# A gated linear-attention block: five small moves in the order of work around the Strassen query stage

## The chip, the core and the metric

The kernel runs on one core of a Trainium2 chip. Its time is device time in microseconds (us), from one launch, median of a few runs. In the profile, PE is the matrix engine (PEld its weight loads), DVE the vector engine, ACT the scalar engine, POOL the GpSimd engine, and SP the engine whose queue issues most DMAs. Each engine takes its own instructions strictly in order and waits on semaphores for the others.

## The reference

All tensors are float32: S = 2048 tokens, D = 640 features, 32 heads of 20, an MLP of width 1536.

```python
xn = layernorm(x)
q, k, v = split(xn @ wqkv)                       # 32 heads x 20
phi(p) = concat(softmax(p), softmax(-p))         # p = q or k times a 20x20 matrix per head
kv = phi_k^T v ;  z = sum_s phi_k                # per head
o = (phi_q kv) / (phi_q z + 1e-6)
s = o @ wo
g = silu(gelu(xn @ w1 + b1) @ w2 + b2)
out = x + s * g
```

## The kernel before

Float32 products are made from float32r parts: a number is split into a high part (copied by ACT) and a low part (original minus high), and a product is three matmul passes, high x high, high x low and low x high (`PASSES`). The head matrices are folded into wq and wk at the start.

**Stages.** (1) Loading and folding of weights, to about 45 us. (2) A loop over 16 token tiles t of 128 tokens, to about 212 us. (3) The Strassen query stage, `query_pair(q)` for q = 4 to 7, to about 250 us; it makes the queries of two tiles (2q and 2q + 1) with seven products instead of eight. (4) Twelve MLP units, each also Strassen, with the normalisation of stored query features beside them. (5) Numerators, output projection and gate.

**A step t of the tile loop** makes the key projection `pk = project(t, wk_s)` and the value projection `value(t)`. Each is 30 matmuls of 320 columns (line 363) into a PSUM tile `pA`, of which there are three; a projection can start when the readers of the tile that had its place are done. From `pk` comes the feature map:

- `feat1` on DVE: maximum (L376), minimum (L377), `p - max` into a slab `e` (L380, the last reader of `pA`), `nr = min - max` (L383); then on POOL the second half of `e` (L384).
- `feat2` on ACT: one exponential over 128x1280 (L393).
- `key_fin`: sums per head on DVE (L401), their reciprocal (L426), and the scaling of `e` on POOL (L406). The result is `phis[t]`.
- `kv_pair(t)`: 64 small matmuls of 40 columns for two tiles (L435), which add phi^T v into one PSUM tile `kv`. They read `phis` and `vs`.

`query(n)` does the same for a query tile, without `key_fin`, and stores `e` in DRAM (L420); queries 0 to 7 are made so, in steps 6 to 9.

**The x for pairs 4 to 7** comes transposed from DRAM (`xr`, 128x1280 for a pair) and is normalised in place: `pair_sub(q)` on POOL (L332), `pair_mul(q)` on DVE (L337). `pair_plain(q)` splits it: three copies on ACT (L283) and three subtractions on DVE (L285), into `xp` and a slab `b`. `t_sums(q)` on POOL (L298, five instructions) makes the Strassen sums `tt`, and `t_split(q)` splits them into `xd`: a copy on ACT (L314) and a subtraction of 128x1152 on POOL (L315).

**The query stage** has seven parts per pair, i = 0 to 6 (L616). Part 1 makes `qY`, which ACT copies (L622); part 3 makes `qV`, for which there is one PSUM place shared with `qY`. DVE adds results at parts 3, 4, 5 and 6 (L625, L627, L629, L632), and POOL adds once at part 1 (L623). After part i, `hooks[i]` runs, which is where the last tile's remaining key work and the making of the first MLP weights (`w1_forms`: L451, L462, L463) are put:

```python
            if i in hooks:
                hooks[i]()
```

Four weight tiles for this stage, `wqs`, are read back from DRAM by `s_back()` in step 15 (L587, on SP's queue).

**What sets the order.** The region is written under a manual schedule: every engine takes its instructions in the order in which the code above emits them. PSUM tiles and slabs are given out by pools; which place a tile gets, and so whom its first writer waits for, follows from the order of releases when the program is built.

Of the kernel before, what the change touches and what calls it, by code (L numbers as in the profile page):

```python
# [16 lines left out]
NT = S // P  # L17
# [18 lines left out]
def _tok(t):  # L36
    q, o = divmod(t, 2)
    h, p = divmod(q, SLOTS)
    return 8 * h + 4 * o + p
# [7 lines left out]
def hedgehog_gated_mlp_kernel(ctx: ExitStack, tc: tile.TileContext, x, xt_in, wqk, bd, wv, wo, w1, b1, w2, b2, out_t):  # L47
# [19 lines left out]
    def xd():  # L67
        if not xds:
            xds.append(xpool.tile([P, 9, 2, CW], F32R, tag="D", name="xd"))
        return xds[0]  # L70
# [10 lines left out]
    def slab(dt, name, shape=(P, 2, D)):  # L81
        return slabs.tile(list(shape), dt, tag="S", name=name)
# [4 lines left out]
    def bankA():  # L87
        return pools["A"].tile([P, 2, 512], F32, tag="A", name="pA")
# [179 lines left out]
    def at(q):  # L268
        return slice((q % SLOTS) * P, (q % SLOTS + 1) * P)
# [10 lines left out]
    def plain(q, o, v):  # L280
        parts = [(xp[:, 0:5, :, at(q)], v)] if o == 0 else [(beside(q), v[:, 0:2]), (xp[:, 5:8, :, at(q)], v[:, 2:5])]
        for dst, src in parts:
            nc.scalar.activation(dst[:, :, 0, :], src, AF.Copy)  # L283
        for dst, src in parts:
            nc.vector.tensor_tensor(dst[:, :, 1, :], src, dst[:, :, 0, :].bitcast(F32), op=OP.subtract)  # L285
# [26 lines left out]
    def t_split(q):  # L312
        tt, dst = tts.pop(q), xd()[:, :, :, at(q)]
        nc.scalar.activation(dst[:, :, 0, :], tt[:], AF.Copy)  # L314
        nc.gpsimd.tensor_tensor(dst[:, :, 1, :], tt[:], dst[:, :, 0, :].bitcast(F32), op=OP.subtract)  # L315
# [23 lines left out]
    def pair_plain(q):  # L339
        for o in range(2):  # L340
            plain(q, o, xrs[q][:, :, o * P:(o + 1) * P])
# [27 lines left out]
    def heads(ps):  # L369
        return ps[:, :, :HALF].rearrange("p a (h d) -> p a h d", d=DH)  # L370

    def feat1(ps, later=None):
        p4 = heads(ps)
        mx = small.tile([P, 2, 16], F32, tag="mx", name="mx")
        mn = small.tile([P, 2, 16], F32, tag="mn", name="mn")
        nc.vector.tensor_reduce(mx[:], p4, axis=AX.X, op=OP.max)  # L376
        nc.vector.tensor_reduce(mn[:], p4, axis=AX.X, op=OP.min)  # L377
        e = slab(F32, "e")[:]
        e5 = e.rearrange("p a (h s d) -> p a h s d", s=2, d=DH)
        nc.vector.tensor_tensor(e5[:, :, :, 0, :], p4, mx[:, :, :, None].to_broadcast([P, 2, 16, DH]),  # L380
                                op=OP.subtract)
        nr = small.tile([P, 2, 16], F32, tag="nr", name="nr")
        last_feat[0] = nc.vector.tensor_tensor(nr[:], mn[:], mx[:], op=OP.subtract)  # L383
        rest = lambda: nc.gpsimd.tensor_tensor(e5[:, :, :, 1, :], nr[:, :, :, None].to_broadcast([P, 2, 16, DH]),  # L384
                                               e5[:, :, :, 0, :], op=OP.subtract)
        if later is None:
            rest()
        else:
            later.append(rest)
        return e.rearrange("p a b -> p (a b)")  # L390

    def feat2(ef):
        nc.scalar.activation(ef, ef, AF.Exp)  # L393
        return ef

    def features(ps):
        return feat2(feat1(ps))

    def head_sums(ef, tag):
        ss = small.tile([P, 64], F32, tag=tag, name=tag)  # L400
        nc.vector.tensor_reduce(ss[:], ef.rearrange("p (g d) -> p g d", d=DH), axis=AX.X, op=OP.add)  # L401
        return ss
# [15 lines left out]
    def query(t):  # L418
        ef = features(project(t, wq_s))
        nc.scalar.dma_start(e_dram[_tok(t)], ef)  # L420
# [3 lines left out]
    def key_fin(ef):  # L424
        ss = head_sums(ef, "rc")
        nc.vector.reciprocal(ss[:], ss[:])  # L426
        scale_heads(ef, ss)
        return ef
# [10 lines left out]
    vs, es, phis, xns, wk_s, wq_s = {}, {}, {}, {}, [], [None] * 4  # L439
# [161 lines left out]
    def query_pair(q, hooks, later):  # L601
        even, odd = bankA(), None
        bank, seen = {"X": even[:, 0, :HALF], "W": even[:, 1, :HALF]}, set()
        r1 = row([P, 2, HALF], F32, "qx")
        r2 = row([P, 2, HALF], F32, "qu")
        for i, (ch, wn, xb, extra) in enumerate(QPARTS):
            if ch in "YV":
                bank[ch] = bankB("q" + ch)[:, :HALF]
            if i == 4:
                odd = bankA()  # L610
                bank["Z"] = odd[:, 0, :HALF]
            mms = [(wn, k, b, xb + k, a) for k in range(2) for a, b in PASSES]
            if extra:
                mms += [(extra[0], 0, b, extra[1], a) for a, b in PASSES]
            for n, (w, k, b, blk, a) in enumerate(mms):
                nc.tensor.matmul(bank[ch], q_x(blk, a, q), q_weight(w, k)[:, b], start=ch not in seen and n == 0,  # L616
                                 stop=n == len(mms) - 1, skip_group_check=True)
            seen.add(ch)
            if i == 0:
                nc.scalar.activation(r1[:, 0], bank["X"], AF.Copy)  # L620
            elif i == 1:
                nc.scalar.activation(r1[:, 1], bank["Y"], AF.Copy)  # L622
                nc.gpsimd.tensor_tensor(r2[:, 0], r1[:, 0], r1[:, 1], op=OP.add)  # L623
            elif i == 3:
                nc.vector.tensor_tensor(r2[:, 1], r2[:, 0], bank["V"], op=OP.add)  # L625
            elif i == 4:
                nc.vector.tensor_tensor(odd[:, 1, :HALF], r2[:, 1], bank["Z"], op=OP.add)  # L627
            elif i == 5:
                nc.vector.tensor_tensor(bank["W"], r2[:, 1], bank["W"], op=OP.add)  # L629
                ee = feat1(even)  # L630
            elif i == 6:
                nc.vector.tensor_tensor(bank["Z"], r2[:, 0], bank["Z"], op=OP.add)  # L632
            if i in hooks:
                hooks[i]()
        return ee, feat1(odd, later)

    def store_e(t, ef):
        nc.scalar.dma_start(e_dram[_tok(t)], feat2(ef))
# [9 lines left out]
    queries = iter(range(NT // 2))  # L648
# [3 lines left out]
    for t in range(6, NT):  # L652
        q = (t + 2) // 2
        pk = project(t, wk_s)
        for u in XIN.get(t, ()):
            x_in(u)
        for u in STATS.get(t, ()):
            pair_stats(u)
        if t in XR:
            load_xr(XR[t])  # L660
        if t in (6, 8):
            spill(t // 2 - 1)
        if t in (8, 10, 12):
            pair_sub(q)
        es[t] = feat1(pk)
        if t == 6:
            pair_stats(10)
            pair_sub(4)
            fold_w(wqT, range(4, KC), "wq", wq_s)
        if t in (6, 8, 10, 12):  # L670
            pair_mul(q)
        if t == 13:
            w1r = load_w1(0)
        if t in (7, 9, 11, 13):
            t_sums((t + 1) // 2)
        if t == NT - 1:
            s_back()
        if t == NT - 1:
            t_split(7)
        vs[t] = value(t)  # L680
        if t < NT - 1:
            feat2(es[t])
            phis[t] = key_fin(es.pop(t))
        if t in (8, 10, 12):
            pair_plain(q)
        if t in (7, 9):
            t_split((t + 1) // 2)
        if t == 12:
            t_split(6)
        if t == 6:  # L690
            query(next(queries))
            query(next(queries))
            pair_plain(4)
        if 7 <= t < 10:
            query(next(queries))
        if t % 2 == 0 and t < NT - 2:
            kv_pair(t - 2)
        if 7 <= t < 10:
            query(next(queries))
    w1f = w1_forms(w1r)  # L700

    def early_rest(q, ea):
        if q == 4:
            phis[NT - 1] = key_fin(es.pop(NT - 1))
        w1g.append(next(w1f))
        if q == 4:
            return
        later.pop(0)()
        store_e(2 * q - 2, ea)

    def late_rest(q, eb):
        if q == 7:
            w1g.append(next(w1f))
        if q > 4:
            store_e(2 * q - 1, eb)

    later, w1g, ea, eb = [], [], None, None
    for q in range(4, 8):
        if q == 7:
            w2r = [load_raw(w2[f * P:(f + 1) * P, :]) for f in range(GF)]  # L720
        ea, eb = query_pair(q, {1: lambda: early_rest(q, ea), 3: lambda: late_rest(q, eb), **({0: lambda: feat2(es[NT - 1])} if q == 4 else {})}, later)
        if q == 4:
            kv_pair(NT - 4)
        if q == 5:
            kv_pair(NT - 2)
            kvr = kv_rest()
# [494 lines left out]
```

## Time and profile before

| | |
|---|---|
| median of 3 runs | 661.41 us (661.08 to 661.45) |
| the profiled execution | 661.31 us, of which its span is 659.6 us |
| PE busy | 649.7 us (99%), 4414 matmul records |
| DVE, ACT, POOL busy | 486.5, 235.0, 390.5 us |
| mean granted PE clock | 0.999 |

In a row of the timeline the first number is the start in us from the span's start, the second the length of the row in us; then engine, line, operation, output and inputs, shapes, and how many instructions are merged in the row. Brackets tell how long the engine was idle just before, and what ended that idle time. The end of a matmul is modelled by the profiler, so a matmul row is best read by its start and by the start of the next one. A row of the waits has who waited for whom, the total in us, how often, and the longest.

### The profile page before, as it was taken

The page shows a single profiled execution, that of the slowest core. Times are in us where ns is not written, and L with a number is a line of the kernel's source. Part 1 is how long each engine was busy: PE and PEld are TensorE (multiplying, and loading weights), DVE is VectorE, ACT ScalarE, POOL GpSimd, SP SyncE. Part 2 cuts the span into 40 slices and gives each one's busy share as a digit, 9 for nine tenths or more (in the row PEclk, how much of TensorE's full clock was granted, in tenths as well). Part 3 has the DMA queues.
Part 4 walks back from the last instruction along what each step waited for, and adds up shares of the span by engine and source line. Part 5 has one row for each costly group of instructions (what it writes and reads, how often), then busy time and mean ns, then how long its engine had stood idle before and what let it go on. Part 6 is the DMA issues. An engine that isn't in the chain of part 4 may idle for free.

```text
span 659.6 us, 11407 instructions
## 1 busy us (share of the span) xinstructions
PE 649.7 (99%) x4414; PEld 564.1 (86%) x4414; DVE 486.5 (74%) x749; ACT 235.0 (36%) x334; POOL 390.5 (59%) x348
## 2 busy tenths in 40 slices
PE   9999999999999999999999999999999999999997
PEld 9999999999999898888888888888888887766866
DVE  5785955898686788668979968759789899852232
ACT  3512523233233346352442444841332424132130
POOL 2755464949566854957768876363472967343321
PEclk9999999999999999999999999999999999999999
DMA  9706092654204287537899799497779399999962
GB/s 351 272 1 172 6 329 108 157 175 137 82 15 147 88 277 264 173 95 264 190 294 314 171 408 327 97 318 258 151 218 242 84 260 201 303 230 244 280 235 81
DMA packets 161408, 132.22 MB, mean 200 GB/s; under 512 B 89170, under 2 KB 127314, under 8 KB 160458
## 3 DMA queue, kind: packets, MB, share of 16 engines
q1 hardware_dynamic: 158618, 119.89, 62.3%
q10 hardware_dynamic: 2736, 11.60, 4.8%
q8 instruction: 35, 0.57, 0.3%
q14 instruction: 19, 0.16, 0.1%
HBM read 83.74 MB, written 47.73 MB: 199 GB/s over the span
## 4 chain that ended last, share of the span: by engine, by line
PE 67%; DVE 8%; POOL 3%; ACT 1%; issue 1%; DMA 0%; DVEq 0%; POOLq 0%
PE pB L810 24%; PE pB L781 22%; PE pB L965 11%; PE pA L616 3%; PE pA L363 3%; PE pB L912 2%; POOL e L384 2%; DVE b L285 1%; DVE rc L401 1%; ACT e L393 1%; DVE xp L285 1%; DVE nr L383 1%; PE qV L616 1%; DVE mx L376 1%; DVE mn L377 1%
## 5 line engine op out<-in xcount | busy, mean ns | idle before, releaser
L810 PE MATMUL pB<-hs,w2s 128*128 128x512 f32 x720 | 165.7, 389 | 0.0
L810 PEld LDWEIGHTS pB<-hs,w2s 128*128 128x128 f32 x720 | 135.0, 188 | 28.8 <-DVE y L819 0.8
L781 PE MATMUL pB<-xp,w1s 128*128 128x512 f32 x324 | 81.3, 389 | 0.0
L781 PE MATMUL pB<-xd,w1s 128*128 128x512 f32 x324 | 79.3, 389 | 0.0
L965 PE MATMUL pB<-oT,wo 128*128 128x512 f32 (+1 forms) x315 | 72.3, 381 | 0.0
L781 PEld LDWEIGHTS pB<-xd,w1s 128*128 128x128 f32 x324 | 60.8, 188 | 12.6
L781 PEld LDWEIGHTS pB<-xp,w1s 128*128 128x128 f32 x324 | 60.7, 188 | 12.7 <-DVE pB L1046 0.2
L406 POOL TENSOR_TENSOR eq<-eq,rc 128x1280 f32<-128x1280 f32 x16 | 37.9, 2368 | 54.3 <-DVE rc L869 37.1
L965 PEld LDWEIGHTS pB<-oT,wo 128*128 128x128 f32 x315 | 57.2, 188 | 13.8 <-PE pB L912 2.5
L393 ACT ACTIVATE e<-e 128x1280 f32<-128x1280 f32 x32 | 40.7, 1272 | 75.0 <-POOL e L384 74.1
L819 DVE TENSOR_TENSOR y<-pB,y 128x512 f32<-128x512 f32 x100 | 63.2, 676 | 1.4 <-PE pB L810 1.4
L406 POOL TENSOR_TENSOR e<-e,rc 128x1280 f32<-128x1280 f32 x16 | 39.0, 2439 | 40.9 <-DVE rc L426 40.6
L384 POOL TENSOR_TENSOR e<-nr,e 128x640 f32<-128x640 f32 x32 | 43.8, 1370 | 31.4 <-DVE nr L383 24.3
L363 PE MATMUL pA<-wv,xp 128*128 128x320 f32 x384 | 59.8, 310 | 1.8 <-DVE nr L383 1.8
L786 ACT ACTIVATE pB<-pB,b1t 128x512 f32<-128x512 f32 x48 | 31.8, 662 | 78.9 <-DVE pB L1046 29.7
L363 PE MATMUL pA<-wk,xp 128*128 128x320 f32 x384 | 59.6, 310 | 0.0
L363 PEld LDWEIGHTS pA<-wv,xp 128*128 128x128 f32 x384 | 56.9, 188 | 2.1 <-issue 2.1
L363 PEld LDWEIGHTS pA<-wk,xp 128*128 128x128 f32 x384 | 56.9, 188 | 0.1
L856 POOL TENSOR_TENSOR ez<-eq,zrep 128x1280 f32<-128x1280 f32 x16 | 47.4, 2960 | 2.5 <-DMA eq<-e_dram 2.5
L463 POOL TENSOR_TENSOR w1s<-raw,w1s 128x640 fp32r<-128x640 f32 (+1 forms) x18 | 26.2, 1454 | 29.8 <-ACT w1s L462 29.8
L401 DVE TENSOR_REDUCE rc<-e 128x64 f32<-128x1280 f32 x16 | 23.7, 1483 | 23.5 <-ACT e L393 23.5
L968 POOL TENSOR_TENSOR xres<-gt,xres 128x256 f32<-128x256 f32 x20 | 14.3, 736 | 35.7 <-DVE gt L967 35.7
(165 smaller groups left out, 1102.7 us busy)
## 6 DMA issues: line engine op xcount, KB each, us to landing
raw<-in_w_dram SPq DMA_DIRECT2D x42, 320.0 KB
e_dram<-e ACTq DMA_DIRECT2D x16, 640.0 KB
eq<-e_dram SPq DMA_DIRECT2D x16, 640.0 KB
phi_t<-eq SPq DMA_DIRECT2D x64, 160.0 KB
phT<-phi_t SPq DMA_DIRECT2D x20, 480.0 KB
xres<-in_xt_dram SPq DMA_DIRECT2D x20, 256.0 KB
xt<-in_x_dram SPq DMA_DIRECT2D x15, 320.0 KB
out_dram<-xres SPq DMA_DIRECT2D x18, 256.0 KB
```

The lines of the kernel that those rows point to most:

```text
L363: nc.tensor.matmul(ps[:, hf, :HALF], stat_x(q, o, k, a), ws[k][:, b, hf * HALF:(hf + 1) * HALF], start=n == 0, stop=n == 3 * KC - 1)
L384: rest = lambda: nc.gpsimd.tensor_tensor(e5[:, :, :, 1, :], nr[:, :, :, None].to_broadcast([P, 2, 16, DH]), e5[:, :, :, 0, :], op=OP.subtract)
L393: nc.scalar.activation(ef, ef, AF.Exp)
L401: nc.vector.tensor_reduce(ss[:], ef.rearrange("p (g d) -> p g d", d=DH), axis=AX.X, op=OP.add)
L406: nc.gpsimd.tensor_tensor(e3, e3, rc[:, :, None].to_broadcast([P, 64, DH]), op=OP.mult)
L616: nc.tensor.matmul(bank[ch], q_x(blk, a, q), q_weight(w, k)[:, b], start=ch not in seen and n == 0, stop=n == len(mms) - 1, skip_group_che ...
L781: nc.tensor.matmul(bank[ch][:], tl[:, a, off + wo_:off + wo_ + P], mov(blk, b), start=new and n == 0, stop=n == len(mms) - 1, skip_group_c ...
L786: nc.scalar.activation(ps, ps, AF.Gelu_apprx_tanh, bias=b1t[:, f:f + 1])
L810: nc.tensor.matmul(ps[:], ws[i][:, b, d * P:(d + 1) * P], hs[o][i][:, a, :], start=i == n == 0, stop=(i, n) == (GF - 1, 2), skip_group_che ...
L819: nc.vector.tensor_tensor(y, ps[:], y, op=OP.add)
L856: nc.gpsimd.tensor_tensor(zv, ef, zf, op=OP.mult)
L965: nc.tensor.matmul(ps[:, mv], w, o[:, mv], start=n == 0, stop=n == 15, skip_group_check=True)
```

## The change

No instruction is added or removed; five groups move.

1. In steps 8, 10 and 12 `pair_plain(q)` stands before `key_fin(t)` instead of after it.
2. `t_split(6)` moves from the end of step 12 to step 13, behind `feat1`. `t_split(7)` moves from step 15 to step 14, behind `feat1`.
3. In step 8 the block of key-value matmuls `kv_pair(6)` moves behind the second query instead of between the two.
4. The last exponential, `feat2(es[15])`, moves from behind part 0 of `query_pair(4)` to behind part 1.
5. The last `key_fin` moves from behind part 1 to behind part 4.

```diff
         es[t] = feat1(pk)
+        if t in (13, 14):
+            t_split(t - 7)
...
-        if t == NT - 1:
-            t_split(7)
         vs[t] = value(t)
         if t < NT - 1:
             feat2(es[t])
-            phis[t] = key_fin(es.pop(t))
         if t in (8, 10, 12):
             pair_plain(q)
+        if t < NT - 1:
+            phis[t] = key_fin(es.pop(t))
         if t in (7, 9):
             t_split((t + 1) // 2)
-        if t == 12:
-            t_split(6)
...
         if 7 <= t < 10:
             query(next(queries))
+        if 7 <= t < 10:
+            query(next(queries))
         if t % 2 == 0 and t < NT - 2:
             kv_pair(t - 2)
-        if 7 <= t < 10:
-            query(next(queries))
...
         if q == 4:
-            phis[NT - 1] = key_fin(es.pop(NT - 1))
+            feat2(es[NT - 1])
         w1g.append(next(w1f))
...
+    def last_key():
+        phis[NT - 1] = key_fin(es.pop(NT - 1))
...
-        ea, eb = query_pair(q, {1: lambda: early_rest(q, ea), 3: lambda: late_rest(q, eb), **({0: lambda: feat2(es[NT - 1])} if q == 4 else {})}, later)
+        ea, eb = query_pair(q, {1: lambda: early_rest(q, ea), 3: lambda: late_rest(q, eb), **({4: last_key} if q == 4 else {})}, later)
```

On DVE in step 8 (steps 10 and 12 read alike), from the normalisation of `xr` to the next feature map; `-` is before, `+` is now:

```order
 L383 TENSOR_TENSOR nr<-mn,mx 128x32
 L337 TENSOR_TENSOR xr<-xr,bc 128x1280
-L401 TENSOR_REDUCE rc<-e 128x64
-L426 RECIPROCAL rc<-rc 128x64
 L285 TENSOR_TENSOR xp<-xr,xp 128x5x128
 L285 TENSOR_TENSOR b_1281<-xr,b_1281 128x2x128
 L285 TENSOR_TENSOR xp<-xr,xp 128x3x128
+L401 TENSOR_REDUCE rc<-e 128x64
+L426 RECIPROCAL rc<-rc 128x64
```

The head sums and their reciprocal moved behind the three subtractions of the split, and with them the POOL scaling (L406) that waits for the reciprocal.

On POOL from the scaling of tile 12 to the sums of pair 7, before:

```order
L406 TENSOR_TENSOR e<-e,rc 128x1280
L315 TENSOR_TENSOR xd<-tt,xd 128x9x128
L384 TENSOR_TENSOR e<-nr,e 128x32x20
L298 TENSOR_TENSOR tt<-xr 128x256 x2
L298 TENSOR_TENSOR tt<-xr,tt 128x256 x2
```

and now:

```order
L406 TENSOR_TENSOR e<-e,rc 128x1280
L384 TENSOR_TENSOR e<-nr,e 128x32x20
L315 TENSOR_TENSOR xd<-tt,xd 128x9x128
L298 TENSOR_TENSOR tt<-xr 128x256 x2
L298 TENSOR_TENSOR tt<-xr,tt 128x256 x2
```

The subtraction of `t_split(6)` changed places with the second half of tile 13's features, for which it now has to wait. That of `t_split(7)` likewise stands two tiles' work earlier, right behind tile 14's L384.

On ACT around the start of the query stage:

```order
 L314 ACTIVATE xd<-tt 128x9x128
 L415 ACTIVATE v<-pA 128x32x20
+L393 ACTIVATE e<-e 128x1280
+L415 ACTIVATE v<-pA 128x32x20
 L620 ACTIVATE qx<-pA 128x320
-L393 ACTIVATE e<-e 128x1280
 L622 ACTIVATE qx<-qY 128x320
+L393 ACTIVATE e<-e 128x1280
```

The last exponential changed places with the copy of `qY`, and the copy of `t_split(7)` stands one tile earlier, ahead of the copy of value tile 14.

## The prediction

> **What bounds the kernel now.** I read the profile's first page for the busy shares, then PE's own waits, then one row by windows for the part behind the change, then the timeline at each wait.
>
> ```profile
> PE 649.7 (99%) x4414; PEld 564.1 (86%) x4414; DVE 486.5 (74%) x749; ACT 235.0 (36%) x334; POOL 390.5 (59%) x348
> ...
> q8 instruction: 35, 0.57, 0.3%
> ...
> PE pA L363 <- DVE nr L383: 2.1, 2, 1.8
> PE qV L616 <- ACT qx L622: 1.6, 1, 1.6
> PE kv L435 <- issue: 0.9, 1, 0.9
> ...
> 250.00:556.00 306.00, 306.00 (x1353) 253.29 (x1352) 251.18 (x365) 126.03 (x187) 200.58 (x143) 1.00 0.79 228
> ```
>
> PE is busy for 649.7 of 659.6 us. Its named waits in the region of the change are three: 2.1 us for DVE in the tile loop, 1.6 us for ACT in the query stage, and 0.9 us inside a key-value block that no semaphore explains. From 250 to 556 us PE has no gap at all (306.00 busy of 306.00). So whatever PE gains before 250 us moves everything behind it forward, as long as that part stays bound by PE; and no work of PE is removed, so these waits are all that can be won.
>
> **The change part by part.** The edits act on three waits of PE. I measure them from start to start, since the rows' ends are modelled.
>
> *Step 8: DVE order, and the key-value block.* The rows of PE, DVE, ACT and POOL there:
>
> ```profile
> 126.36 0.81 DVE L380 TENSOR_TENSOR e<-pA,mx 128x640 f32<-128x640 f32 x1
> 128.47 0.83 PE L435 MATMUL kv<-e,v 128*32 128x40 f32 x67
> 130.19 1.47 PE L435 MATMUL kv<-e,v 128*32 128x40 f32 x61 [0.88 <-issue]
> 131.59 2.02 PE L363 MATMUL pA<-wq,b 128*128 128x320 f32 x12
> 132.69 0.72 ACT L283 ACTIVATE xp<-xr 128x640 fp32r<-128x640 f32 x1
> 132.82 1.49 DVE L401 TENSOR_REDUCE rc<-e 128x64 f32<-128x1280 f32 x1 [2.47 <-ACT e L393]
> 134.81 0.76 DVE L285 TENSOR_TENSOR xp<-xr,xp 128x640 fp32r<-128x640 f32 x1
> 135.04 2.75 POOL L406 TENSOR_TENSOR e<-e,rc 128x1280 f32<-128x1280 f32 x1 [3.43 <-DVE rc L426]
> 135.49 2.58 DVE L285 TENSOR_TENSOR b<-xr,b 128x256 fp32r<-128x256 f32 x1
> 136.09 1.92 PE L363 MATMUL pA<-wk,b 128*128 128x320 f32 x12
> 137.99 0.55 DVE L285 TENSOR_TENSOR xp<-xr,xp 128x384 fp32r<-128x384 f32 x1
> 139.93 0.81 DVE L380 TENSOR_TENSOR e<-pA,mx 128x640 f32<-128x640 f32 x1
> 140.88 1.99 PE L363 MATMUL pA<-wv,b 128*128 128x320 f32 x12 [0.23 <-DVE nr L383]
> ...
> 163.04 1.39 PE L435 MATMUL kv<-e,v 128*32 128x40 f32 x128
> ```
>
> The second subtraction of the split has 256 elements a partition and takes 2.58 us, though the third, with 384, takes 0.55: it ends (138.07) just behind POOL's L406 (137.79), which began when the reciprocal was done. A DVE operation with two SBUF inputs and a POOL operation exclude each other here. With the split first, POOL has nothing to do beside it, because L406 waits for a reciprocal that now comes later. DVE then runs: first subtraction from the end of its ACT copy at 133.41, 0.68 (134.81 to 135.49); the second, at most 0.47 (the third takes 0.55 less 0.08 of overlap); sums and reciprocal 1.99 (132.82 to 134.81); from the third subtraction to the end of that L380, 2.75 (137.99 to 140.74). The end of the feature map's L380 for the first query is then 139.30 instead of 140.74, though DVE now waits for the copies. The value projection of tile 9 followed L380 by 0.14, so it can start at 139.44.
>
> PE's side of it: the key-value block takes 3.19 us (128.47 to 131.66), against 1.39 for the same block in step 10: 1.80 more, most of it the stall in the middle. The key projection of tile 9 starts at 136.09 and its 30 matmuls need 4.40 (six take 0.88 in the rows of the query stage below, 213.07 to 213.95), so PE was ready at 140.49 and lost 0.39. Moving the block is free for its neighbours: the second query needs the place of tile 8's keys, whose last reader ended at 127.17, before 128.47. If the stall is gone, PE is ready at 140.49 - 1.80 = 138.69 and waits until 139.44: gain 1.44. If it stays, PE is ready at 140.49 and DVE no longer matters: gain 0.39. Nothing in the rows names the stall's cause, so these are the ends; I take 1.44, since of the eight key-value blocks only this one stalls so long, and it leaves its place by 30 matmuls.
>
> *Steps 12 to 14: the split again, and `t_split(6)`.*
>
> ```profile
> 188.38 0.74 ACT L283 ACTIVATE xp<-xr 128x640 fp32r<-128x640 f32 x1
> 190.56 2.75 POOL L406 TENSOR_TENSOR e<-e,rc 128x1280 f32<-128x1280 f32 x1 [3.44 <-DVE rc L426]
> 192.51 4.56 PE L363 MATMUL pA<-wk,xp 128*128 128x320 f32 x30
> 192.71 0.70 ACT L415 ACTIVATE v<-pA 128x640 f32<-128x640 f32 x1 [1.81 <-PE pA L363]
> 193.28 2.87 POOL L315 TENSOR_TENSOR xd<-tt,xd 128x1152 fp32r<-128x1152 f32 x1
> 193.52 3.05 DVE L285 TENSOR_TENSOR xp<-xr,xp 128x384 fp32r<-128x384 f32 x1
> 197.95 0.81 DVE L380 TENSOR_TENSOR e<-pA,mx 128x640 f32<-128x640 f32 x1
> 198.91 4.64 PE L363 MATMUL pA<-wv,xp 128*128 128x320 f32 x30 [1.83 <-DVE nr L383]
> ```
>
> Here the split is caught twice, by L406 and then by L315 of `t_split(6)` (3.05 us for what takes 0.55). Tile 13's L380 ends at 198.76, and value tile 14, which needs the place that it frees, starts at 198.91. PE was ready at 192.51 + 4.40 = 196.91: 2.00 lost. Now both POOL operations stand behind the split. With the sum of step 8, L380 ends 189.12 + 0.68 + 0.47 + 1.99 + 2.75 = 195.01, before 196.91. Besides, in the built order value tile 14 gets another place and waits for the copy of value tile 13, which ended at 193.41. Both ways the 2.00 goes. What is late next is `t_split(6)`, which now waits for tile 13's L384; its cover is priced below.
>
> *The start of the query stage.*
>
> ```profile
> 213.07 1.04 PE L616 MATMUL qY<-wqs,xd 128*128 128x320 f32 x6
> 213.95 1.48 PE L616 MATMUL pA<-wq,xp 128*128 128x320 f32 x9
> 215.40 1.27 ACT L393 ACTIVATE e<-e 128x1280 f32<-128x1280 f32 x1 [1.69 <-POOL e L384]
> 216.57 0.42 ACT L622 ACTIVATE qx<-qY 128x320 f32<-128x320 f32 x1
> 217.04 1.14 PE L616 MATMUL qV<-wqs,xd 128*128 128x320 f32 x6 [1.61 <-ACT qx L622]
> ```
>
> The copy of `qY` stands behind the last exponential, which waits for POOL; `qV` needs the copy. Part 2 has nine matmuls at 0.147 (0.88/6), so PE was ready at 215.27 and lost 1.77. With the copy first, it starts when `qY` is done, 214.11, and ends by 214.6: the 1.77 goes. The exponential and `key_fin` of tile 15 come later; only the block of tiles 14 and 15 reads them, a whole query pair later, so they cost PE nothing. On DVE the 1.99 of sums and reciprocal now lies between L627 and L629.
>
> **The sum.** 1.44 + 2.00 + 1.77 = 5.21. The profiled execution took 661.31, 0.10 under the median of 661.41: 661.31 - 5.21 = 656.10.
>
> What covers the edits costed at nothing is POOL and SP:
>
> ```profile
> 196.18 9.48 SPq L587 DMA_DIRECT2D wqs<-s_dram  x4
> ...
> 199.01 1.28 POOL L384 TENSOR_TENSOR e<-nr,e 128x640 f32<-128x640 f32 x1 [2.86 <-DVE nr L383]
> ...
> 211.52 2.37 POOL L406 TENSOR_TENSOR e<-e,rc 128x1280 f32<-128x1280 f32 x1 [3.71 <-DVE rc L426]
> ...
> 218.03 0.89 POOL L623 TENSOR_TENSOR qu<-qx 128x320 f32<-128x320 f32 x1
> ...
> 220.66 1.04 PE L616 MATMUL pA<-wqs,xp 128*128 128x320 f32 x6
> ...
> 328.25 0.60 ACT L797 ACTIVATE x<-pB 128x512 f32<-128x512 f32 x1 [0.37 <-PE pB L781]
> ```
>
> The first `wqs` load is released by the end of `t_split(6)`: 196.18 before; now tile 13's L384 (195.15 + 1.28) and L315 (2.87) end near 199.3. PE reads it from 213.07 less 3.44, so 10 us remain; all four loads were issued within 9.48 us before and none was waited for. L623 stands behind everything on POOL; it and DVE's L625 and L627 must be done before part 6 (220.66, now 215.45). POOL starts this stretch with tile 13's L384 at 195.15 instead of 199.01, and 1.44 earlier still if step 8's gain is passed on: 5.3, about the 5.2 that PE asks for. But the first L315, 2.87, now lies inside the stretch. It has to come out of idle time, and the row of tile 14's scaling shows 3.71: enough by 0.8.
>
> **The rivals.**
> 1. *The stall inside the key-value block stays.* It is tied to the place in PE's instruction stream, and that place stays inside the block. For it: the rows call it "issue". Against: seven other blocks run without it. Sum: 0.39 + 2.00 + 1.77 = 4.16, so 657.15. The Trainium skill (Runtime: NRT & Kernel Launch, section Instruction fetch mechanics) says that instructions stream in blocks of 16 KiB and that crossing a block is mostly hidden. The trace agrees on the size (35 packets, 0.57 MB: 16 KB each). By that rule the stall is no fetch, moving the block need not remove it, and the sum is this rival's; no row here shows what else it would be.
> 2. *POOL becomes late at the query stage.* Step 8's 1.44 is not passed on, or the idle time is not where L315 needs it; part 6 waits 1 to 2 us: 657.1 to 658.1. For it: the margin is 0.8. Against: most of POOL's work there is released by engines that come forward too.
> 3. *The gain is given back in the MLP units.* At 328.25 the ACT copy that frees PE's next place had waited only 0.37 for PE. If the transfer ahead of it kept its clock time, up to 4.8 of the 5.21 would return there: 660.9, no difference. Against: its work is started by engines that PE itself releases, so it moves forward too.
> 4. *Slower: the third `wqs` load.* It waits for the sums of pair 7, which stand behind the later `t_split(6)`. Part 4 reads it at 217.04 + 9 x 0.147 = 218.36, now 213.15. Each us that it lands later than 213.15 costs one, and from 218.36 on the kernel is slower than before; landing at 220 gives 661.31 + 1.64 = 662.95. For it: the order on POOL. Against: the loads were issued by 205.66, and the sums would have to end some 4 us later than they did even if 12.7 us (205.66 to 218.36) is the time that a load needs; by the starts above they end no later.
>
> **How the numbers follow.** Forecast 0.52; rival 1 0.25; rival 2 0.10; rival 3 0.07; rival 4 0.05; anything else faster 0.01. A difference under 0.2% (1.3 us) can hardly be told from none. Faster by more: 0.52 + 0.25 + 0.10 + 0.01 = 0.88; within: 0.07; slower: 0.05. The predicted time is 656.1. The range: down to all of PE's losses gone, 661.31 - (1.80 + 0.39 + 2.00 + 1.77) = 655.35, and 0.15 for scatter, 655.2; up to rival 2's end, 658.1, rounded to 658.2. It holds 0.87.
>
> **What would show it.** In the profile after: the second and third subtraction of the split at 0.4 to 0.6 us in steps 8, 10 and 12; no wait of value tile 14 on DVE; no wait of `qV` on ACT; value tile 9 near 139.4 and `qV` near 211.8. A key-value block of 3.1 us would be rival 1, a gap before part 6 rival 2, gaps of PE between 250 and 556 us rival 3, a wait of part 4 for a DMA rival 4. I am wrong if the starts of 250 us and later move by less than 4 us.

## The result

| | before | after |
|---|---|---|
| median | 661.43 us (661.08 to 661.49) | 655.87 us (655.47 to 656.12) |
| the profiled execution | 661.31 us, span 659.6 | 655.47 us, span 653.8 |
| PE busy | 649.7 us | 648.0 us |
| DVE busy | 486.5 us | 476.0 us |

The ratio of after to before is 0.9916, with a 95% interval of 0.9899 to 0.9934. The medians differ by 5.56 us, the two profiled executions by 5.84.

The page's busy line of the changed kernel, PE's waits, and the row by windows for the part behind the change:

```profile
PE 648.0 (99%) x4414; PEld 563.0 (86%) x4414; DVE 476.0 (73%) x749; ACT 235.3 (36%) x334; POOL 389.5 (60%) x348
```

```profile
PE pA L499 <- PEq L1213: 0.8, 1, 0.8
PE pA L363 <- DVE e L380: 0.6, 1, 0.6
PE pB L921 <- DVE y L821: 0.4, 1, 0.4
```

```profile
250.00:556.00 306.00, 305.76 (x1351) 250.34 (x1349) 251.36 (x362) 125.00 (x188) 201.22 (x142) 1.00 0.81 228
```

The 2.1 us for DVE, the 1.6 us for ACT and the 0.9 us inside the key-value block are gone; of the region of the change one wait of 0.6 is left. The long stretch behind it is as full as before, so what was won there stays won. DVE is 10.5 us less busy though it does the same work: most of the difference is time in which its subtractions stood waiting for POOL, which the profile counts as busy (the second subtraction alone took 2.16 us less in each of steps 8, 10 and 12).

The timeline of the changed kernel at the three places, step 8, steps 12 to 14, and the start of the query stage (the changed code is two lines longer, so that the MLP's L781 is L783 here):

```profile
132.79 1.39 PE L435 MATMUL kv<-e,v 128*32 128x40 f32 x128
134.11 2.03 PE L363 MATMUL pA<-wk,b 128*128 128x320 f32 x12
...
134.19 0.42 DVE L285 TENSOR_TENSOR b<-xr,b 128x256 fp32r<-128x256 f32 x1
134.99 1.48 DVE L401 TENSOR_REDUCE rc<-e 128x64 f32<-128x1280 f32 x1
137.20 2.37 POOL L406 TENSOR_TENSOR e<-e,rc 128x1280 f32<-128x1280 f32 x1 [5.59 <-DVE rc L426]
138.38 0.81 DVE L380 TENSOR_TENSOR e<-pA,mx 128x640 f32<-128x640 f32 x1
139.34 1.99 PE L363 MATMUL pA<-wv,b 128*128 128x320 f32 x12 [0.56 <-DVE e L380]
...
187.45 0.42 DVE L285 TENSOR_TENSOR b<-xr,b 128x256 fp32r<-128x256 f32 x1
187.78 0.55 DVE L285 TENSOR_TENSOR xp<-xr,xp 128x384 fp32r<-128x384 f32 x1
191.64 0.81 DVE L380 TENSOR_TENSOR e<-pA,mx 128x640 f32<-128x640 f32 x1
194.25 2.69 POOL L315 TENSOR_TENSOR xd<-tt,xd 128x1152 fp32r<-128x1152 f32 x1
195.25 4.56 PE L363 MATMUL pA<-wv,xp 128*128 128x320 f32 x30
...
210.41 0.44 ACT L622 ACTIVATE qx<-qY 128x320 f32<-128x320 f32 x1 [0.44 <-PE qY L616]
211.38 1.27 ACT L393 ACTIVATE e<-e 128x1280 f32<-128x1280 f32 x1 [0.54 <-POOL e L384]
211.43 0.89 POOL L623 TENSOR_TENSOR qu<-qx 128x320 f32<-128x320 f32 x1
211.53 1.04 PE L616 MATMUL qV<-wqs,xd 128*128 128x320 f32 x6
213.12 0.49 DVE L625 TENSOR_TENSOR qu<-qu,qV 128x320 f32<-128x320 f32 x1 [3.19 <-PE qV L616]
213.99 0.49 DVE L627 TENSOR_TENSOR pA<-qu,pA 128x320 f32<-128x320 f32 x1 [0.38 <-PE pA L616]
215.05 1.04 PE L616 MATMUL pA<-wqs,xp 128*128 128x320 f32 x6
...
243.17 1.55 PE L783 MATMUL pB<-xp,w1s 128*128 128x512 f32 x6
```

The second subtraction takes 0.42 at both places instead of 2.58 and 2.58, the third 0.55 instead of 3.05 in step 12. Value tile 9 starts at 139.34 instead of 140.88 (1.54 earlier), value tile 14 at 195.25 instead of 198.91 (3.66), `qV` at 211.53 instead of 217.04 (5.51), and the first MLP matmul, which in the kernel before stood here:

```profile
249.06 1.55 PE L781 MATMUL pB<-xp,w1s 128*128 128x512 f32 x6
```

5.89 earlier. Of this 0.08 was there before the change began: the projection of step 8's first query starts at 123.90 instead of 123.98.

### The profile page after: what moved, and what is told of

Same layout as the page of the kernel before. It is cut to its first block, busy times and chain, and to the rows that moved or that the text cites. A ratio compares the mean times of both kernels' runs of the same rounds, so it can differ in the third digit from the quotient of the medians.

```text
span 653.8 us, 11408 instructions
## 1 busy us (share of the span) xinstructions
PE 648.0 (99%) x4414; PEld 563.0 (86%) x4414; DVE 476.0 (73%) x749; ACT 235.3 (36%) x334; POOL 389.5 (60%) x348
## 4 chain that ended last, share of the span: by engine, by line
PE 76%; DVE 3%; DMA 0%; issue 0%; POOL 0%; ACT 0%; DVEq 0%; SPq 0%; ACTq 0%
PE pB L812 24%; PE pB L783 22%; PE pB L967 11%; PE pA L363 10%; PE pA L616 4%; PE pB L914 2%; PE kv L435 1%; PE qV L616 1%; DVE y L821 1%; PE pB L921 1%; PE qY L616 1%; DMA phi_t<-eq 0%; POOL e L384 0%; DVE nr L383 0%; DVE wolh L891 0%
## 5 line engine op out<-in xcount | busy, mean ns | idle before, releaser
L783 PE MATMUL pB<-xp,w1s 128*128 128x512 f32 x324 | 81.4, 389 | 0.0
L783 PE MATMUL pB<-xd,w1s 128*128 128x512 f32 x324 | 79.3, 389 | 0.0
L783 PEld LDWEIGHTS pB<-xd,w1s 128*128 128x128 f32 x324 | 60.8, 188 | 12.6
L783 PEld LDWEIGHTS pB<-xp,w1s 128*128 128x128 f32 x324 | 60.7, 188 | 12.7 <-DVE pB L1048 0.2
L406 POOL TENSOR_TENSOR eq<-eq,rc 128x1280 f32<-128x1280 f32 x16 | 37.9, 2372 | 54.2 <-DVE rc L871 37.1
L406 POOL TENSOR_TENSOR e<-e,rc 128x1280 f32<-128x1280 f32 x16 | 37.9, 2368 | 45.9 <-DVE rc L426 45.6
L384 POOL TENSOR_TENSOR e<-nr,e 128x640 f32<-128x640 f32 x32 | 43.8, 1371 | 22.4 <-DVE nr L383 19.3
```

Source lines behind the costliest of these rows:

```text
L406: nc.gpsimd.tensor_tensor(e3, e3, rc[:, :, None].to_broadcast([P, 64, DH]), op=OP.mult)
L783: nc.tensor.matmul(bank[ch][:], tl[:, a, off + wo_:off + wo_ + P], mov(blk, b), start=new and n == 0, stop=n == len(mms) - 1, skip_group_c ...
```

## The experiments

PE's losses are told as in the prediction: from start to start, less what the same matmuls take elsewhere. The block is the key-value block of tiles 6 and 7, from its first matmul to the next one behind it. It has 128 matmul records, 64 for each of its two tiles; undisturbed it takes 1.32 or 1.33 us.

| kernel | block | v9 waits | v14 waits | qV waits | part 6 waits | median |
|---|---|---|---|---|---|---|
| before | 3.12 | 0.39 | 2.00 | 1.77 | 0 | 661.43 |
| edit 1 alone | 3.26 | 0 | 0 | 0.94 | 0 | 657.71 |
| edit 3 alone | 1.33 | 2.24 | 0.81 | 1.77 | 0 | 661.40 |
| edits 4, 5 alone | 3.32 | 0.40 | 1.98 | 0 | 0 | 661.12 |
| after | 1.32 | 0.72 | 0 | 0 | 0 | 655.87 |
| after less edit 3 | 3.44 | 0 | 0 | 0 | 0 | 657.09 |
| after less edits 4, 5 | 1.33 | 0.74 | 0 | 1.49 | 0 | 657.20 |
| after less edit 5 | 1.32 | 0.72 | 0 | 0 | 0.77 | 656.29 |
| after less edit 2 | 1.33 | 0.50 | 0 | 0 | 1.54 | 657.56 |
| after, and key_fin(8) later | 1.32 | 0 | 0 | 0 | 0 | 654.61, again 654.82 |

### The first edit alone

```diff
         if t < NT - 1:
             feat2(es[t])
-            phis[t] = key_fin(es.pop(t))
         if t in (8, 10, 12):
             pair_plain(q)
+        if t < NT - 1:
+            phis[t] = key_fin(es.pop(t))
```

> The kernel before with the first edit alone: the split of x ahead of the head sums in steps 8, 10 and 12. Theory: the second and third subtraction take 0.4 to 0.55 us in all three steps; in step 8 the key-value block stalls as before and only 0.39 is won, in step 12 the whole 2.00 goes, though t_split(6) keeps its place, since on POOL it stands behind L406, which now waits for the later reciprocal; qV still waits about 1.7 for ACT. 661.43 - 2.39 = 659.0. Rival A (the stall is not tied to the block's place): 1.4 instead of 0.39 in step 8, 658.0. Rival B (the 2.00 needs the move of t_split(6) too): 661.43 - 0.39 = 661.0.

657.71 us, ratio 0.9946 (0.9930 to 0.9963): faster than the theory's 659.0. Its PE rows in step 8 and at `qV`:

```profile
128.50 0.86 PE L435 MATMUL kv<-e,v 128*32 128x40 f32 x70
130.55 1.28 PE L435 MATMUL kv<-e,v 128*32 128x40 f32 x58 [1.19 <-issue]
...
213.71 1.14 PE L616 MATMUL qV<-wqs,xd 128*128 128x320 f32 x6 [0.78 <-ACT qx L622]
```

The block stalls as before, and value tile 14 waits for nothing: the order on DVE alone removes the 2.00, and the move of `t_split(6)` isn't needed for it (rivals A and B fall). What the theory had wrong is `qV`, which waits 0.94 and not 1.7: POOL's L384, the exponential and the copy came forward by more than PE did, 3.33 (217.04 to 213.71).

### The third edit alone

```diff
         if 7 <= t < 10:
             query(next(queries))
+        if 7 <= t < 10:
+            query(next(queries))
         if t % 2 == 0 and t < NT - 2:
             kv_pair(t - 2)
-        if 7 <= t < 10:
-            query(next(queries))
```

> The kernel before with the third edit alone: the key-value block of step 8 behind both queries. Theory: the block takes 1.33 instead of 3.19, but value tile 9 still waits for L380, which ends near 140.74 with the old order on DVE, so it starts at 140.9 as before and waits about 2.2: no change, 661.4. Rival A (the block alone sets that time): 1.4 to 1.8 are won, 659.6 to 660.0. Rival B (the stall stays inside the block): the block takes 3.2, no change either, and PE's wait for DVE stays 0.4.

661.40 us, ratio 0.9999 (0.9989 to 1.0008): the theory's number, with the block at 1.33 and value tile 9 starting at 140.63. PE's row there, and the row by windows just behind it (the last three columns are the granted clock, the DMA share and GB/s):

```profile
140.63 3.50 PE L363 MATMUL pA<-wv,b 128*128 128x320 f32 x12 [2.08 <-DVE nr L383]
```

```profile
140.60:144.20 3.60, 3.57 (x14) 3.60 (x15) 3.53 (x10) 1.27 (x1) 2.52 (x3) 0.53 0.04 18
```

PE only waits longer for the same L380. After that wait the granted clock was about half for some 3.4 us, which cost PE another 1.5; the wait of value tile 14 was shorter by about as much (0.81 instead of 2.00), since DVE sets its start. That is how a loss of PE ahead of a wait for DVE costs nothing.

### The fourth and fifth edit alone

```diff
         if q == 4:
-            phis[NT - 1] = key_fin(es.pop(NT - 1))
+            feat2(es[NT - 1])
...
+    def last_key():
+        phis[NT - 1] = key_fin(es.pop(NT - 1))
...
-        ea, eb = query_pair(q, {1: lambda: early_rest(q, ea), 3: lambda: late_rest(q, eb), **({0: lambda: feat2(es[NT - 1])} if q == 4 else {})}, later)
+        ea, eb = query_pair(q, {1: lambda: early_rest(q, ea), 3: lambda: late_rest(q, eb), **({4: last_key} if q == 4 else {})}, later)
```

> The kernel before with the fourth and fifth edit alone. Theory: qV no longer waits for ACT and starts near 215.27 instead of 217.04, but L623 still stands behind L315 on POOL (ends 217.97 before), so that L625 and L627 end near 219.95 and part 6 waits until about 220.05 instead of starting at 218.89; before it started at 220.66. Of the 1.77, 0.6 is left: 660.8. Rival A (POOL is not late): 1.77, 659.7. Rival B (all of it is lost again): 661.4.

661.12 us, ratio 0.9994 (0.9984 to 1.0004): no difference that can be told from none. Rival A falls. The profiled execution loses the gain at another place than the theory said:

```profile
198.87 6.16 PE L363 MATMUL pA<-wv,xp 128*128 128x320 f32 x30 [1.82 <-DVE nr L383]
204.87 1.92 PE L363 MATMUL pA<-wk,b 128*128 128x320 f32 x12
...
218.05 0.88 POOL L623 TENSOR_TENSOR qu<-qx 128x320 f32<-128x320 f32 x1
...
219.56 0.50 DVE L627 TENSOR_TENSOR pA<-qu,pA 128x320 f32<-128x320 f32 x1
...
220.27 1.04 PE L616 MATMUL pA<-wqs,xp 128*128 128x320 f32 x6
```

Value tile 14 takes 6.00 (198.87 to 204.87) instead of 4.48 before, because the clock is halved after the wait of 1.98; the same second in that kernel and in the kernel before:

```profile
200.00:201.00 1.00, 1.00 (x5) 1.00 (x5) 0.00 (x0) 0.72 (x1) 1.00 (x3) 0.50 0.00 0
```

```profile
200.00:201.00 1.00, 1.00 (x9) 1.00 (x8) 0.00 (x0) 0.68 (x1) 1.00 (x3) 1.00 0.00 0
```

So PE reached part 6 only at 220.27. L627 ended near 220.06, and a PE that was 1.5 earlier would have waited for it: the ceiling that the theory named is there in the rows, but this execution did not run against it. These are two ways to nearly the same time, and the other executions bear it out. The mean granted clock was 0.997 in this one; of the ten executions five had 0.996 or 0.997 and five 0.999 or 1.0, and they took 661.15 and 661.13 us on average.

### The change without its third edit

The diff is the third edit's, turned round.

> The changed kernel with the key-value block of tiles 6 and 7 put back between the two queries of step 8; all else as changed. Theory (the stall belongs to the block's place): the block takes about 3.2 us again instead of the 1.32 (132.79 to 134.11) of the changed kernel, PE is ready for value tile 9 near 140.4, behind the end of DVE's L380 (139.20), so that PE no longer waits for DVE there and the kernel loses 140.4 - 139.34 = 1.1 us: about 657.0. Rival A (the stall came from what the other engines did in the old order, or was a single execution's): the block takes 1.33, value tile 9 waits 0.6 to 0.7 for DVE as in the changed kernel, 655.9.

657.09 us, ratio 0.9935 (0.9921 to 0.9950), as the theory had it (657.0). PE's rows in step 8:

```profile
128.87 0.83 PE L435 MATMUL kv<-e,v 128*32 128x40 f32 x67
130.18 0.22 PE L435 MATMUL kv<-e,v 128*32 128x40 f32 x1 [0.47 <-issue]
131.02 1.36 PE L435 MATMUL kv<-e,v 128*32 128x40 f32 x60 [0.62 <-issue]
132.31 2.03 PE L363 MATMUL pA<-wq,b 128*128 128x320 f32 x12
```

The stall is back, and value tile 9 no longer waits: PE comes later than DVE. In step 8 the first and the third edit need each other: the third alone is worth nothing, here it is worth 1.22.

### The change without its fourth and fifth edit, and without the fifth

The diff of the first kernel is that of the two edits, turned round.

> The changed kernel with the fourth and fifth edit undone: the last exponential behind part 0 of the first query pair, the last key_fin behind part 1. Theory: the exponential waits for POOL's L384 of tile 15 (ends 211.35 in the changed kernel), runs 1.27, and only then is qY copied (0.44): qV starts near 213.0 instead of 211.53, a loss of 1.5: 657.3. Rival A (with POOL's work moved forward by the other edits the exponential is done early enough): 655.9. Rival B (the old wait in full): 1.77, and L401 and L426 ahead of L625 delay part 6 besides by up to 0.7: 658.3.

657.20 us, ratio 0.9941 (0.9926 to 0.9956), the theory's 657.3:

```profile
212.19 0.42 ACT L622 ACTIVATE qx<-qY 128x320 f32<-128x320 f32 x1
...
212.66 1.14 PE L616 MATMUL qV<-wqs,xd 128*128 128x320 f32 x6 [1.33 <-ACT qx L622]
```

The copy of `qY` stands behind the exponential again, and `qV` waits 1.49. With the exponential in its new place but the sums right behind it:

```diff
         if q == 4:
             feat2(es[NT - 1])
+            phis[NT - 1] = key_fin(es.pop(NT - 1))
...
-        ea, eb = query_pair(q, {1: lambda: early_rest(q, ea), 3: lambda: late_rest(q, eb), **({4: last_key} if q == 4 else {})}, later)
+        ea, eb = query_pair(q, {1: lambda: early_rest(q, ea), 3: lambda: late_rest(q, eb)}, later)
```

> The changed kernel with the fifth edit alone undone: the last key_fin behind part 1, right after the last exponential. Theory: DVE's L401 and L426 (1.99 together) then start when the exponential ends, 212.65, and are done near 214.65, ahead of L625, which ran at 213.12 in the changed kernel; L625 and L627 follow near 215.6 and part 6 of the first pair starts near 215.75 instead of 215.05: a loss of 0.7, 656.6. Rival A (the sums fit into DVE's idle time): 655.9. Rival B (POOL's L406, 2.37 from 214.9, keeps L627 out): part 6 near 217.4, 658.2.

656.29 us, ratio 0.9923 (0.9908 to 0.9937):

```profile
215.60 0.49 DVE L627 TENSOR_TENSOR pA<-qu,pA 128x320 f32<-128x320 f32 x1
...
216.15 1.15 PE L616 MATMUL pA<-wqs,xp 128*128 128x320 f32 x6 [0.61 <-DVE pA L627]
```

Part 6 waits 0.77 for L627, as the theory had it (0.7), and POOL's L406, which ran from 215.30, did not keep L627 out. So without the fifth edit the fourth would lose a part of its gain: 0.77 by the rows, 0.42 by the medians, whose ranges overlap (655.84 to 656.75 and 655.47 to 656.12).

### The change without its second edit

```diff
         es[t] = feat1(pk)
-        if t in (13, 14):
-            t_split(t - 7)
...
             s_back()
+        if t == NT - 1:
+            t_split(7)
...
             t_split((t + 1) // 2)
+        if t == 12:
+            t_split(6)
```

> The changed kernel with the second edit undone: t_split(6) at the end of step 12, t_split(7) in step 15. Theory: value tile 14 waits for nothing, as in the changed kernel (the run of the first edit alone has no such wait), but at the query stage the subtraction L315 of pair 7 (2.68) stands on POOL between tile 15's L384 (ends 211.35) and L623: L623 ends near 215.15, L627 near 216.1, and part 6 starts near 216.2 instead of 215.05: a loss of 1.15, 657.0. Rival A (POOL has idle time for it): 655.9. Rival B (value tile 14's wait of 2.0 comes back): 659.0 or, with the loss at part 6 hidden behind it, 657.9.

657.56 us, ratio 0.9942 (0.9928 to 0.9957), some more than the theory's 657.0:

```profile
211.58 2.68 POOL L315 TENSOR_TENSOR xd<-tt,xd 128x1152 fp32r<-128x1152 f32 x1
...
215.87 0.50 DVE L627 TENSOR_TENSOR pA<-qu,pA 128x320 f32<-128x320 f32 x1
...
216.42 1.16 PE L616 MATMUL pA<-wqs,xp 128*128 128x320 f32 x6 [1.37 <-DVE pA L627]
```

The mechanism is the theory's: L315 of pair 7 stands between tile 15's L384 and L623 on POOL, and part 6 waits 1.54 for what comes of it. (In the whole change this L315 moved ahead of two operations of POOL, tile 14's L406 and tile 15's L384, which is one tile's work and not two.) So the move of `t_split` wins nothing at the place where the wait of value tile 14 was, and keeps 1.5 us from being lost 20 us later.

### What the stall in the block hangs on

Two kernels were built on the change without its third edit. The first has 64 more matmul records ahead of the block:

```diff
         for u in (t, t + 1):
+            if u == 5:
+                kv_acc(u, phis[u], vs[u])
             kv_acc(u, phis.pop(u), vs.pop(u))
```

> The changed kernel with the key-value block of step 8 back between the queries (as in the run of that edit alone) and the matmuls of tile 5 made twice in step 6, so that tile 5 counts double and 64 matmul records more (0.66 us) lie ahead of the block in PE's instruction stream. It asks what the stall is tied to; so far it began at record 67 to 70 of the 128 of the block, 129.1 to 129.7 us. Theory I (a place in PE's instruction stream): it comes 64 records earlier in the block, at record 3 to 6, or is gone. Theory D (the time at which the DMA engines stand still: store packets that start at 128.2 to 129 take 2.2 us instead of 0.2): it begins at 129.1 to 129.7 on whatever record runs then and ends by 131. Theory T (the place inside the block, or the data of tile 7): record 67 to 70 again, whenever that is.

The second leaves out the feature stores of queries 2 and 3 and stores the features of query 1 three times instead:

```diff
     def query(t):
         ef = features(project(t, wq_s))
-        nc.scalar.dma_start(e_dram[_tok(t)], ef)
+        for u in {0: (0,), 1: (1, 2, 3), 2: (), 3: ()}.get(t, (t,)):
+            nc.scalar.dma_start(e_dram[_tok(u)], ef)
```

> The changed kernel with the key-value block of step 8 back between the queries, and without the two stores of query features that ACT issues at 124.9 and 126.6; in their place the features of query 1 are stored three times in step 6, so that two tiles get another tile's features. Theory D (the PE stall comes with the DMA standstill behind these stores): no DMA runs at 128 to 131, the block takes 1.33 instead of 3.4, value tile 9 waits for DVE as in the changed kernel. Theories I and T (place in the stream or in the block): the block takes 3.2 to 3.4 as before.

They took 658.49 and 657.91 us; both lost PE time elsewhere, so only the block is read. Its row and the one other that matters, of the first, and its row in the second:

```profile
101.58 0.56 PE L363 MATMUL pA<-wk,b 128*128 128x320 f32 x2 [1.92 <-issue]
...
132.65 1.39 PE L435 MATMUL kv<-e,v 128*32 128x40 f32 x128
133.97 2.02 PE L363 MATMUL pA<-wq,b 128*128 128x320 f32 x12
```

```profile
131.04 1.39 PE L436 MATMUL kv<-e,v 128*32 128x40 f32 x128
132.37 1.88 PE L363 MATMUL pA<-wq,b 128*128 128x320 f32 x11
```

No stall in either. In the second the block has the same place in PE's stream and the same data as in the kernel that stalled, so theories I and T fall: neither the place in the stream nor the block itself is enough. The rows by windows from 128.5 to 131.5 us, of before, of after and of the second kernel:

```profile
128.50:131.50 3.00, 1.99 (x129) 1.68 (x128) 1.85 (x2) 0.00 (x0) 2.87 (x4) 1.00 0.65 80
```

```profile
128.50:131.50 3.00, 3.00 (x22) 3.00 (x21) 1.84 (x2) 0.00 (x0) 2.87 (x4) 1.00 0.58 75
```

```profile
128.50:131.50 3.00, 3.00 (x67) 2.81 (x68) 3.00 (x4) 0.87 (x2) 2.96 (x1) 1.00 0.06 3
```

In before and after the DMA engines are busy for 0.65 and 0.58 of that time and move only 80 and 75 GB/s, after 381 and 387 in the 2.5 us before it. In the second kernel next to nothing is under way. The block stalls in each kernel in which it starts at 128.31 to 128.87 (before, edit 1 alone, edits 4 and 5 alone, after less edit 3, and the run below), and in none in which it starts at 131.04 or later. That fits theory D, but does not show it: the second kernel's block came later too, at 131.04, since PE had waited about 2 us ahead of value tile 8, so the empty stretch and the later time were not told apart.

It isn't shown either how a standstill of transfers reaches matmuls that wait for no transfer. After's 320-column matmuls run through the same stretch without a gap. A late load of instructions is an obvious rival, and no run was made for it; the profile's two instruction queues, q8 and q14, have no packet that starts from 128.5 to 131.8 us in any of the five kernels that stall, so none is seen to end the stop. The first kernel has another stop, which theory D does not fit: behind a key-value block of 192 records, PE stops for 1.92 us, until 101.58, among 320-column matmuls, with no semaphore to wait for. In the 1.7 us up to it the DMA engines moved 375 GB/s, and one packet of q8 starts between 99.1 and 100.2. The cause of both stops stays open.

A last run was to ask where the standstill comes from:

```diff
-            nc.sync.dma_start(st_dram[q].rearrange("i p s -> p i s"), pst[0][:])
+            for u in {4: (4, 5), 5: ()}.get(q, (q,)):
+                nc.sync.dma_start(st_dram[u].rearrange("i p s -> p i s"), pst[0][:])
```

> The changed kernel with the key-value block of step 8 back between the queries, and without the small store that SP issues at 126.35 for the statistics of pair 5 (L324, 256 packets of 8 bytes, which run at 127.5 to 128.6); the statistics of pair 4 are stored for both pairs instead, so that pair 5 is normalised with another pair's. The stores of query features stay. It asks whether the standstill of the DMA engines, 128.5 to 131, comes from that store. Theory S (it does): no packet of the feature stores takes over 0.5 us, the key-value block takes 1.33, and value tile 9 waits for DVE as in the changed kernel. Rival (the feature stores end so by themselves, or other engines hold the memory up): packets of 2.2 us near 128.8 and a block of 3.2 to 3.4 as in the run with the block moved alone. The loads of L326, L293 and L294 no longer wait for the store and come 4 us earlier in both cases.

This run took out the wrong store: the small store at 126 is that of pair 6, and that of pair 5, which was taken out, is issued near 111. The store meant was still there (issued at 125.95), the standstill too, and the block took 3.40 (656.89 us). Theory S was not tried and stays open; the run is one more repeat of the stall.

### One more move: key_fin of step 8

The wait of 0.72 that the change leaves in step 8 is for the first query's L380, with 1.99 of sums ahead of it on DVE.

```diff
-        if t < NT - 1:
+        if t < NT - 1 and t != 8:
             phis[t] = key_fin(es.pop(t))
...
         if 7 <= t < 10:
             query(next(queries))
+        if t == 8:
+            phis[t] = key_fin(es.pop(t))
         if 7 <= t < 10:
             query(next(queries))
```

> The changed kernel with one more move: in step 8 key_fin (L401, L426, L406) stands behind the first of the two queries instead of ahead of both. Theory: the first query's L380 ends 1.99 earlier, near 137.2, before PE is ready for value tile 9 (139.34 less the 0.72 that it lost there), and that wait goes: 655.15. Rival (the wait only moves on, to the projections that need the second query's L380 or the places that tile 8's keys hold back): 655.9.

654.61 us (654.30 to 655.13), ratio 0.9898 (0.9883 to 0.9913):

```profile
136.79 0.81 DVE L380 TENSOR_TENSOR e<-pA,mx 128x640 f32<-128x640 f32 x1
...
138.83 1.92 PE L363 MATMUL pA<-wv,b 128*128 128x320 f32 x12
```

L380 ends at 137.60 and PE starts when it is ready; no new wait appears. It was timed again:

> The same kernel as the one with key_fin of step 8 behind the first query, timed again in more rounds: 654.6, which is a ratio of 0.990 to the kernel before, if the 654.61 of the first runs was not chance; 655.2 if only the 0.72 that value tile 9 waited was won; 655.9 if nothing was.

654.82 us (654.50 to 655.33), ratio 0.9899 (0.9882 to 0.9915). The ranges of both runs lie below that of the change (655.47 to 656.12), though they were not timed side by side with it, and the intervals of the ratios overlap (0.9899 to 0.9934 for the change). The rows of step 8 explain 0.72 of the 1.05 to 1.26.

## Why the prediction was right

The forecast was 656.1, the measured time 655.87, by the mechanism that it named; each step of its sum came out within 0.15. That the totals agree within 0.3 is partly luck: in the rows of the profiled executions 5.81 was won up to the first MLP matmul, not 5.21, and the medians differ by 5.56.

- **Step 8, 1.44.** Measured 1.46 (1.54, less the 0.08 from before). Value tile 9 was forecast at 139.44 and started at 139.34; its wait of 0.75 (138.69 to 139.44) was 0.72. It was right to take the end at which the stall goes, but the ground given, that only this block stalls, was thin. What the runs show is that the block stalls when it starts at 128.31 to 128.87, in a stretch in which transfers all but stand still, and not when it starts later; moving it behind the second query makes it start at 132.79. Rival 1 took the stall as tied to the block's place in the stream. The Trainium skill (Runtime: NRT & Kernel Launch, section Instruction fetch mechanics) says that crossing a 16 KiB block of instructions is mostly hidden. The prediction read in it that the stall is no fetch and that moving the block need not help; no instruction packet was seen in the stall, and moving the block helped nonetheless.
- **Steps 12 to 14, 2.00.** Value tile 14 gained 2.12, of which 0.12 are a pause in an earlier key-value block. Of the two grounds given, the order on DVE is enough (edit 1 alone). The end of L380 was forecast at 195.01 and came at 192.45: all rows ahead of it were left at their old clock time, though the gain of step 8 and PE's earlier work moved them. That erred on the safe side here.
- **Query stage, 1.77.** 1.85 with 0.08 of value tile 14's slow start in the kernel before. It would not have come by itself: the prediction costed `t_split`'s move at nothing and weighed it only as a load on POOL (rival 2). The run without it shows that it takes L315 out of POOL's way and keeps 1.54 from being lost at part 6, and the run without the fifth edit 0.77 more. The forecast holds because all five edits were summed together; a sum by single edits would have been wrong by these. In this part the number is better than the reason given for it.
- **POOL's margin, 0.8.** POOL's L623 ended at 212.32, and DVE's L625, which reads its result, began at 213.12, when PE had `qV` done: POOL had 0.80 to spare there. L627 then waited 0.38 for PE, ended at 214.48, and part 6 began at 215.05: another 0.57. So POOL could have come about 1.75 later (0.80 + 0.38 + 0.57, an estimate from these rows) before part 6 waited; that the forecast margin has the same 0.8 is chance, since it was worked out from the idle time ahead of tile 14's L406.
- **Rival 3** did not come: 305.76 of 306.00 between 250 and 556 us. **Rival 4** did not either: the first `wqs` load was forecast near 199.3 and went out at 196.97.
- **What the sum left out** is 0.38 between `qV` and the MLP and the two bits above: the first matmuls after a wait take 0.08 to 0.10 longer in all, and pauses of 0.13 and 0.28 next to key-value blocks went away. They had no place in the sum because no row names a cause for them.

## What to carry to other kernels

Read a wait together with the next one behind it on the other engines. Here edit 1, edit 3, and edits 4 and 5 were worth 3.7, 0.0 and about 0.3 us alone; edit 3, edits 4 and 5, and edit 2 were worth 1.2, 1.3 and 1.7 us when taken away from the whole: each removed wait showed the next, and an edit that removed none kept the next from forming. Where operations of two engines exclude each other, as DVE's subtractions and POOL's L406 and L315 do here, look at the order in which they are released, and not only at the sum of their work: the same instructions took 10.5 us less of DVE.

## What was not expected of the hardware

**The clock after a wait of 2 us.** In three profiled executions the granted clock went to 0.50 for about 3.4 us behind an idle PE of 1.98 to 2.24 us (edit 3 alone, edits 4 and 5 alone, and the kernel with more records), and cost PE 1.5 us or a little more each time; in the profiled execution of the kernel before it stayed at 1.00 behind a wait of 2.00. Executions without a profile have a mean granted clock on record, 0.997 in the three with the slow stretch and 0.999 in that of the kernel before. By this measure (an estimate) the slow stretch came in 20 of 40 executions of the kernel before, 6 of 10 of edit 3 alone, 5 of 10 of edits 4 and 5 alone, 2 of 4 of the kernel with more records, and in none of the changed kernel. In the first three, where PE waits for another engine again further on and so can make up for it, the average times with it and without it differ by 0.2 us or less; in the kernel with more records by 1.3.

The Trainium skill (TensorE: Matmul & The Clock Gate, Part 1: The HAM clock gate) has the half clock and a free-running window of about 3.4 us, after one of which spent idle the clock falls. The half agrees with the 0.50; the waits here were shorter than the window and still the clock fell, so the measurement decides: a wait of 2 us can cost PE 1.5 us more, and need not.

**A standstill of transfers.** From 128.5 to 131.5 us the DMA engines move 65 to 126 GB/s, after 344 to 394 in the 2.5 us ahead, in each kernel of this case except the one without the two feature stores. What causes it, and whether it is what stops a dense block of short matmuls, stays open.
